# Attention kernel on one core: first loads in halves and earlier, a second load behind a memset, and 64-query pieces ahead of 192-query pieces in one of three score steps

## The chip, the cores and the metric

The program runs on one core of one Trainium2 chip. The metric is device time in microseconds (us) for the whole program. "Span" is the time from the first to the last instruction of the profiled execution; it lies about 1.8 us under the measured time.

## The reference

```python
B, H, Sq, Sk, D = 16, 32, 192, 1024, 128        # q, k, v: bf16, normal * 0.05

def reference(q, k, v):
    scale = q.shape[-1] ** -0.5
    scores = jnp.einsum("bhqd,bhkd->bhqk", q, k) * scale
    p = _softmax(scores, axis=-1)
    return jnp.einsum("bhqk,bhkd->bhqd", p, v)
```

There are 512 heads with 192 queries and 1024 keys each. Reading K, V and q and writing the output moves 319 MB.

## The kernel before

Four heads make a group, so there are 128 groups, numbered x. The 4 x 192 queries times 1024 keys of a group are worked in three steps; a step has a number f, and b = f mod 3 says which third of a group it is. For each group

- SP loads K (1 MB), q (192 KB) and V (1 MB) into one of five buffers each,
- DVE transposes K in three pieces (`turn_k`) and q once, three steps ahead of use,
- POOL reorders the K pieces (`order`) and spreads V (`spread`),
- PE makes the scores (`qk`, row tiles of 32), ACT takes the exponential straight out of PSUM (one activation of 512 columns, here called the exp of step f, then one of 1536), PE makes output and row sum (`pv`, four steps later), and DVE divides (`onorm`).

PE runs the following. `take(s, c)` is an instruction of its own: it waits until a semaphore is c or more and takes c off.

```python
CUTS = (                      # per step: groups of pieces (key tile, first query, last query)
    (((0, 0, 192),), ((1, 0, 192),), ((2, 0, 128),)),
    (((3, 0, 192), (2, 128, 192)), ((4, 0, 192), (5, 0, 64))),      # the middle step, b = 1
    (((5, 64, 192),), ((6, 0, 192),), ((7, 0, 192),)),
)
def qk(f):
    x, b = divmod(f, 3)
    if b == 0:
        take(s_qt, 1)
    take(s_kt, 1)
    take(s_e1, 1)
    for group in CUTS[b]:
        for w in range(4):
            for g, (t, n0, n1) in enumerate(group):
                for a in range(4):
                    ins = pe.matmul(...)          # 32 rows x 128 keys, n1 - n0 queries
    ins.then_inc(s_qk, 1)

def pv(s, part=(0, 32)):
    x, i = divmod(s, 3)
    if part[0] == 0:
        if i == 0:
            take(s_e3, 3)
            take(s_vp, 2)
        ...                                       # last steps cut
            take(s_on, 1)
    for n in range(*part):
        ins = pe.matmul(...)                      # 32 matmuls of 129 columns
    ins.then_inc(s_pv, 1)

with nc.Fori(0, NF // (3 * R), engines=[PE], ...):    # six steps a turn
    pv(-PRE - 1 - LAG, (CLOSE, 32))
    for f in range(-PRE, 3 * R - PRE):
        qk(f)
        pv(f - LAG, (0, CLOSE if f == 3 * R - PRE - 1 else 32))     # LAG = 4
```

`pv` with i = 0 always stands in a step with b = 1. The first steps work on blank data that POOL, DVE and ACT set, until the first K has come. SP starts with two waits, one for the first real score step, one for a blank output step:

```python
load_k(0)
load_k(1)
load_q(e, 1)
for n in range(2, NKN):
    if n == 2:
        e.wait_ge(s_qk, PRE + 1)        # first wait: scores of step 0 are done
    load_v(n - 2)
    if n == 2:
        e.wait_ge(s_pv, BLANK - 2)      # second wait: output matmuls of step 1 are done
    load_k(n)
    load_q(e, n)
for n in range(NQ):                     # ... then V, K, q of the next groups for ever
```

Of the kernel before, what the change touches and what calls it, by code (L numbers as in the profile page):

```python
# [30 lines left out]
def _general_path(nc, q, k, v, out, redo, hints, stored, G=16, NS=2, LAGS=(2, 4, 5, 7), ROUTES=(R_W, R_W, R_EA)):  # L31
# [376 lines left out]
U32 = mybir.dt.uint32  # L408
# [3 lines left out]

CUTS = (
    (((0, 0, 192),), ((1, 0, 192),), ((2, 0, 128),)),
    (((3, 0, 192), (2, 128, 192)), ((4, 0, 192), (5, 0, 64))),
    (((5, 64, 192),), ((6, 0, 192),), ((7, 0, 192),)),
)
PIECES = ((0, 6), (6, 12), (12, 16))
# [2 lines left out]
def _attention_kernel(nc, q, k, v, out):  # L421
# [5 lines left out]
    T = SK // 128  # L427
# [6 lines left out]
    PRE = 1  # L434
    BLANK = LAG + 1 + PRE

    AHEAD = 3
    NKN, NVS, NKT, NVP = 5, 5, 2, 2
# [5 lines left out]
    kf = k.rearrange("b h s d -> (b h) s d")  # L444
    vf = v.rearrange("b h s d -> (b h) s d")
# [5 lines left out]
    with ExitStack() as outer:  # L451
        redo = outer.enter_context(nc.sbuf_tensor("redo", [1, 1], mybir.dt.int32))

        def sem(name):
            return outer.enter_context(nc.semaphore(name))

        s_set = sem("f_set")
        s_one = sem("f_one")
        s_out = sem("f_out")
        s_kn = [sem("f_kn%d" % i) for i in range(NKN)]  # L460
        s_qn = [sem("f_qn%d" % i) for i in range(NKN)]
        s_v = [sem("f_v%d" % i) for i in range(NVS)]
# [5 lines left out]
        s_qk = sem("f_qk")  # L468
        s_e1 = sem("f_e1")
        s_e3 = sem("f_e3")  # L470
        s_pv = sem("f_pv")
# [7 lines left out]
        with ExitStack() as es:  # L479
            def sb(name, shape, dt):  # L480
                return es.enter_context(nc.sbuf_tensor(name, shape, dt))
# [5 lines left out]
            kn = sb("f_kn", [128, NKN, 2048], U32)  # L487
# [7 lines left out]
            vs = sb("f_vs", [128, NVS, 4, T * D], BF16)  # L495
            vp = sb("f_vp", [128, NVP, 4 * T, VB], BF16)
# [17 lines left out]
            def store(e, i):  # L514
                so = i % NSO
                x, c = stores[i]
                if x + c == NQ:
                    e.wait_ge(s_fin, 1)
                else:
                    e.wait_ge(s_rc, 3 * (x + c) + 1)  # L520
                e.dma_start(
                    of[4 * x:4 * x + 4 * c].rearrange("(a x) (p j) d -> (x p) a (j d)", x=2, j=3),
                    ob[:, so, 0:6 * c, :].rearrange("p (a j) d -> p a (j d)", j=3),
                ).then_inc(s_st[so], 16)
# [4 lines left out]
            def load_q(e, x):  # L529
                e.dma_start(  # L530
                    qn[:, x % NKN, :],
                    qf[4 * x:4 * x + 4].rearrange("a (j u) d -> (a j) (u d)", u=6).bitcast(U32),
                ).then_inc(s_qn[x % NKN], 16)
# [3 lines left out]
            def hint(eng):  # L537
                hints[eng.engine] = eng.mark_branch_hint_location()

            @block.sync  # L540
            def _(e):
                def load_k(x):
                    if x >= NKN:
                        e.wait_ge(s_kx, 3 * (x - NKN) + 3)
                    e.dma_start(
                        kn[:, x % NKN, :],
                        kf[4 * x:4 * x + 4].rearrange("a (j r) d -> (a j) (r d)", r=32).bitcast(U32),
                    ).then_inc(s_kn[x % NKN], 16)

                def load_v(x):  # L550
                    if x >= NVS:
                        e.wait_ge(s_pv, 3 * (x - NVS) + 2 + BLANK)
                    e.dma_start(
                        vs[:, x % NVS, :, :],
                        vf[4 * x:4 * x + 4].rearrange("a (m t) d -> m a (t d)", t=T),
                    ).then_inc(s_v[x % NVS], 16)

                load_k(0)
                load_k(1)
                load_q(e, 1)  # L560
                for n in range(2, NKN):

                    if n == 2:
                        e.wait_ge(s_qk, PRE + 1)
                    load_v(n - 2)
                    if n == 2:
                        e.wait_ge(s_pv, BLANK - 2)
                    load_k(n)
                    load_q(e, n)
                for n in range(NQ):  # L570
                    if n == NQ // 2:
                        hint(e)
                    if n + NKN - 2 < NQ:
                        load_v(n + NKN - 2)
                    if n + NKN < NQ:
                        load_k(n + NKN)
                        load_q(e, n + NKN)
                for i in range(len(store_at), len(stores)):
                    store(e, i)
# [4 lines left out]
            @block.gpsimd  # L584
            def _(gp):
                gp.memset(ones[:], 1.0).then_inc(s_one, 1)  # L586

                def set_v(part):
                    return gp.memset(part.bitcast(U32), 0x3F803F80)  # L589

                set_v(vp[:, 0, 0:2 * T].rearrange("p a d -> p (a d)")).then_inc(s_set, 1)
                set_v(vp[:, 0, 2 * T:].rearrange("p a d -> p (a d)")).then_inc(s_out, 1)
                set_v(vp[:, 1].rearrange("p a d -> p (a d)")).then_inc(s_vp, 2)

                def order(g):
                    x, b = divmod(g, 3)
                    lo, hi = PIECES[b]
                    gp.wait_ge(s_kx, g + 1)
                    if x >= NKT - 1 and b == 0:
                        gp.wait_ge(s_qk, 3 * (x - NKT) + 3 + PRE)  # L600
                    gp.tensor_copy(  # L601
                        kt[:, x % NKT].bitcast(U32).rearrange("p U (j s u) c -> p U j s (u c)", s=2, u=2)[:, lo:hi],
                        kx[:, x % 2].rearrange("p (U s j u) -> p U j s u", s=2, j=32, u=2)[:, lo:hi],
                    ).then_inc(s_kt, 1)

                def spread(x, i):
                    if i == 0:
                        gp.wait_ge(s_v[x % NVS], 16 * (x // NVS + 1))
                        gp.wait_ge(s_pv, 3 * (x - NVP) + 3 + BLANK)
                    gp.tensor_copy(  # L610
                        vp[:, x % NVP, 2 * T * i: 2 * T * i + 2 * T, 0:D].bitcast(U32),
                        vs[:, x % NVS, 2 * i: 2 * i + 2, :].rearrange("p a (t d) -> p (a t) d", d=D).bitcast(U32),
                    ).then_inc(s_vp, 1)

                for x in range(NQ + 1):
                    if x == NQ // 2:
                        hint(gp)
                    if x < NQ:
                        for b in range(3):
                            order(3 * x + b)  # L620
                    if x >= 1:
                        for i in range(2):
                            spread(x - 1, i)
# [84 lines left out]
            def _(dve):  # L708
# [10 lines left out]
                for z in range(2):  # L719
                    ins = clear(low[:, z, :, 2, :])  # L720
                ins.then_inc(s_out, 1)
                dve.wait_ge(s_out, 3)
                dve.sem_inc(s_on, LAG + 1 + PRE)
                where = {}
                for i, (x0, c) in enumerate(stores):
# [3 lines left out]
                def turn_k(g):  # L729
                    x, b = divmod(g, 3)  # L730
                    lo, hi = PIECES[b]
                    if b == 0:
                        dve.wait_ge(s_kn[x % NKN], 16 * (x // NKN + 1))
                    if x >= 2:
                        dve.wait_ge(s_qk, 3 * (x - 2) + b + 1 + PRE)
                    dve.transpose(  # L736
                        kx[:, x % 2].rearrange("p (U s j u) -> p s u U j", s=2, j=32, u=2)[:, :, :, lo:hi],
                        kn[:, x % NKN].rearrange("p (s u U i) -> p s u U i", s=2, u=2, i=32)[:, :, :, lo:hi],
                    ).then_inc(s_kx, 1)
# [30 lines left out]
                def check(lo, hi, i, part):  # L770
# [9 lines left out]
                    dve.wait_ge(s_dv, cnt[0])  # L780

                turn_k(0)
                turn_q(0)
                for g in range(1, 5):
                    turn_k(g)
                turn_q(1)
                for f in range(NF + LAG + 1):
                    s = f - LAG - 1
                    if f == NF // 2:
                        hint(dve)  # L790
                    if s >= 0:
                        onorm(s)
                        if 0 <= s - EARLY < 3:
                            check(0, 2 * EARLY, 0, s - EARLY)
                    g = f + AHEAD
                    if 5 <= g < NF:
                        x, b = divmod(g, 3)
                        if b == 2 and x >= 2:
                            turn_q(x)
                        turn_k(g)  # L800
# [37 lines left out]
def bass_standalone__mha_softmax__near_ridge_kernel(  # L838
    nc: bass.Bass,
    q: bass.AP,  # L840
    k: bass.AP,
    v: bass.AP,
    out: bass.AP,
):
    _attention_kernel(nc, q, k, v, out)
# [28 lines left out]
```

## Time and profile before

| | before |
|---|---|
| time, median of 3 runs | 819.46 us (819.17 to 820.69) |
| span of the profiled run | 816.9 us |
| PE busy | 99% |
| steps b = 0, 1, 2 in mid-run | 2.06, 2.10, 2.05 us; 6.218 us for a group |
| DMA, 40 slices | 90% or more of all 16 engines in slices 2 to 39 |

The page of the kernel before opens with the span and then gives busy time by engine. In the rows of its 40-slice part a digit is the busy share of a slice in tenths.

```profile
span 816.9 us, 71709 instructions
PE 806.7 (99%) x32996; PEld 717.5 (88%) x32996; DVE 599.7 (73%) x1293; ACT 749.8 (92%) x772; POOL 550.7 (67%) x648
...
DMA  7999999999999999999999999999999999999992
```

PE and DMA are both full, so either can be the limit. Apart from the last slice, where the loads are over, the start is the only place where both have holes. In the windows view of the kernel before, each line is a stretch of one us with the busy time of PE, weight loads, DVE, ACT and POOL, then the granted TensorE clock, the DMA share and GB/s. The DMA share adds up the times of the packets, so it can pass 1.

```profile
9.00:10.00 1.00, 1.00 (x50) 0.89 (x47) 0.58 (x1) 0.00 (x0) 0.94 (x2) 1.00 0.08 30
10.00:11.00 1.00, 1.00 (x36) 0.91 (x40) 0.76 (x1) 0.96 (x2) 0.49 (x1) 1.00 0.10 23
11.00:12.00 1.00, 1.00 (x66) 0.87 (x64) 1.00 (x2) 0.97 (x1) 0.71 (x1) 1.00 0.89 82
...
14.00:15.00 1.00, 1.00 (x52) 0.84 (x42) 0.00 (x0) 0.16 (x2) 0.00 (x0) 1.00 1.55 377
15.00:16.00 1.00, 1.00 (x43) 0.91 (x40) 0.00 (x0) 1.00 (x2) 0.38 (x1) 1.00 0.39 125
```

The last two figures matter: DMA stands nearly still from 9 to 11 us, starts again slowly, and dips once more at 15 us. The timeline of SP in the kernel before tells why; its columns are start, duration, engine, line, operation, and how many were merged.

```profile
10.03 0.38 SPq L553 DMA_DIRECT2D f_vs<-in_v_dram  x1
13.86 0.33 SPq L545 DMA_DIRECT2D f_kn<-in_k_dram  x1
...
14.71 1.64 SPq L553 DMA_DIRECT2D f_vs<-in_v_dram  x1
16.39 0.51 SPq L545 DMA_DIRECT2D f_kn<-in_k_dram  x1
```

K0 and K1 were issued at 0.81 and 1.26 us. V0 (10.03) and K2 (13.86) are issued behind the two waits. V1 (14.71) and K3 (16.39) come after K2 in program order.

The exp activations in mid-run (timeline of ACT, lines of the 512-column activation; the longer one is left out). Their starts are 2.06 and 2.10 us apart; the second interval is the middle step; a bracket gives the idle time before the instruction and what ended it.

```profile
299.00 0.60 ACT L828 ACTIVATE f_pt<-f_s 128x512 bf16<-128x512 f32 x1
...
301.06 0.60 ACT L828 ACTIVATE f_pt<-f_s 128x512 bf16<-128x512 f32 x1
...
303.16 0.60 ACT L828 ACTIVATE f_pt<-f_s 128x512 bf16<-128x512 f32 x1 [0.16 <-PE f_s L646]
```

Two more lines of the timeline show it:

```profile
26.79 0.42 DVE L761 TENSOR_TENSOR f_ob<-f_o,f_rinv 128x256 bf16<-128x256 f32 x1
...
27.36 1.10 PE L673 MATMUL f_o<-f_vp,f_pt 128*64 128x129 bf16 x32 [1.23 <-PEq L629]
```

### The profile page before, as it was taken

How to read it: one execution, taken by the hardware profiler on the slowest of the kernel's cores; microseconds unless marked ns; L12 is line 12 of the kernel's file. 1: busy time of each engine (PE TensorE's matmuls, PEld its weight loads, DVE VectorE, ACT ScalarE, POOL GpSimd, SP SyncE). 2: the span in 40 equal slices, each digit the busy share in tenths (PEclk: the TensorE clock that was granted, in tenths of full speed). 3: DMA queues.
4: the chain of work that ended last, by engine and by line, in shares of the span. 5: the costliest groups of instructions: out<-in, count | busy, mean ns of one | idle time of the engine just before them, and what ended most of it. 6: DMA issues, size and time to landing. Idle time of an engine off the chain costs nothing. (4 is left out here: it accounts for less than half of the span.)

```text
span 816.9 us, 71709 instructions
## 1 busy us (share of the span) xinstructions
PE 806.7 (99%) x32996; PEld 717.5 (88%) x32996; DVE 599.7 (73%) x1293; ACT 749.8 (92%) x772; POOL 550.7 (67%) x648
## 2 busy tenths in 40 slices
PE   8999999999999999999999999999999999999997
PEld 6888888888888888888888888888888888888886
DVE  4777777777777777777777777777777777777775
ACT  6899999999999999999999999999999999999995
POOL 5667766766776676677667666766766676676664
PEclk9999999999999999999999999999999999999999
DMA  7999999999999999999999999999999999999992
GB/s 269 401 402 405 410 403 406 408 403 406 409 401 407 408 403 409 408 402 409 407 403 408 407 403 407 405 405 400 397 406 403 382 411 397 389 404 387 402 368 70
DMA packets 138294, 319.16 MB, mean 391 GB/s; under 512 B 7184, under 2 KB 56336, under 8 KB 121872
## 3 DMA queue, kind: packets, MB, share of 16 engines
q1 hardware_dynamic: 105376, 294.22, 91.9%
q10 hardware_dynamic: 32880, 24.58, 9.0%
q14 instruction: 32, 0.26, 0.1%
q8 instruction: 6, 0.10, 0.0%
HBM read 293.60 MB, written 25.17 MB: 390 GB/s over the span
## 5 line engine op out<-in xcount | busy, mean ns | idle before, releaser
L831 ACT ACTIVATE f_pt<-f_s 128x1536 bf16<-128x1536 f32 x384 | 554.9, 1445 | 0.0
L601 POOL COPY f_kt<-f_kx 128x768 uint32<-128x768 uint32 (+1 forms) x384 | 301.0, 784 | 254.2 <-DVE f_kx L736 254.1
L673 PE MATMUL f_o<-f_vp,f_pt 128*64 128x129 bf16 x12368 | 425.8, 222 | 2.9 <-PEq L629 1.9
L646 PE MATMUL f_s<-f_qt,f_kt 32*128 32x192 bf16 (+1 forms) x20528 | 423.2, 226 | 2.4 <-PEq L629 1.8
L673 PEld LDWEIGHTS f_o<-f_vp,f_pt 128*64 128x64 bf16 x12368 | 366.1, 110 | 55.2 <-issue 28.1
L646 PEld LDWEIGHTS f_s<-f_qt,f_kt 32*128 32x128 bf16 x20528 | 348.5, 92 | 38.9 <-issue 3.1
L736 DVE STREAM_TRANSPOSE f_kx<-f_kn 128x768 uint32<-128x768 uint32 (+1 forms) x384 | 334.0, 870 | 15.7 <-DMA f_kn<-in_k_dram 15.3
L828 ACT ACTIVATE f_pt<-f_s 128x512 bf16<-128x512 f32 x384 | 229.3, 597 | 58.7 <-PE f_s L646 25.6
L610 POOL COPY f_vp<-f_vs 128x1024 uint32<-128x1024 uint32 x256 | 259.9, 1045 | 1.8 <-DMA f_vs<-in_v_dram 1.8
L757 DVE RECIPROCAL f_rinv<-f_o 128x2 f32<-128x2 f32 x381 | 64.9, 170 | 183.2 <-PE f_o L673 183.0
L761 DVE TENSOR_TENSOR f_ob<-f_o,f_rinv 128x256 bf16<-128x256 f32 x381 | 161.7, 424 | 13.3 <-DVE f_rinv L757 0.3
L745 DVE STREAM_TRANSPOSE f_qt<-f_qn 128x384 uint32<-128x384 uint32 x128 | 73.1, 571 | 0.0
L814 ACT ACTIVATE f_pt<-f_ones 128x1536 f32<-128x1536 bf16 x3 | 4.2, 1472 | 0.0
L589 POOL MEMSET f_vp<- 128x1088 uint32 (+1 forms) x3 | 3.8, 1309 | 0.0
L673 PE MATMUL f_s<-f_vp,f_pt 128*64 128x129 bf16 x96 | 3.1, 220 | 0.2 <-PEq L629 0.2
L673 PEld LDWEIGHTS f_s<-f_vp,f_pt 128*64 128x64 bf16 x96 | 2.9, 110 | 0.3 <-issue 0.3
L814 ACT ACT_TABLE_LOAD x1 | 1.3, 1283 | 1.2 <-PEq L859 1.2
L686 PE MATMUL f_o<-f_ones 128*128 128x512 bf16 x2 | 1.0, 622 | 1.1 <-POOL f_ones L586 1.1
L710 DVE MEMSET f_pt<- 128x256 uint32 x4 | 1.1, 272 | 0.9 <-PEq L859 0.9
L703 PE MATMUL f_o<-f_bad,f_ones 128*1 128x1 bf16 x1 | 0.2, 164 | 1.3 <-DVEq L803 1.3
L757 DVE RECIPROCAL f_rinv<-f_s 128x2 f32<-128x2 f32 x3 | 0.5, 170 | 1.2 <-PE f_s L673 1.2
L703 PEld LDWEIGHTS f_o<-f_bad,f_ones 128*1 128x1 bf16 x1 | 0.1, 79 | 1.4 <-DVEq L803 1.4
(15 smaller groups left out, 6.5 us busy)
## 6 DMA issues: line engine op xcount, KB each, us to landing
f_kn<-in_k_dram SPq DMA_DIRECT2D x128, 1024.0 KB, 18.1
f_vs<-in_v_dram SPq DMA_DIRECT2D x128, 1024.0 KB, 16.3
f_qn<-in_q_dram SPq DMA_DIRECT2D x127, 192.0 KB, 14.2
out_dram<-f_ob ACTq DMA_DIRECT2D x62, 384.0 KB, 9.5
out_dram<-f_ob SPq DMA_DIRECT2D x1, 384.0 KB, 3.1
out_dram<-f_ob SPq DMA_DIRECT2D x2, 192.0 KB, 2.0
f_qn<-in_q_dram ACTq DMA_DIRECT2D x1, 192.0 KB, 5.2
```

The source lines that it names most:

```text
L589: return gp.memset(part.bitcast(U32), 0x3F803F80)
L601: gp.tensor_copy(kt[:, x % NKT].bitcast(U32).rearrange("p U (j s u) c -> p U j s (u c)", s=2, u=2)[:, lo:hi], kx[:, x % 2].rearrange("p (U ...
L610: gp.tensor_copy(vp[:, x % NVP, 2 * T * i: 2 * T * i + 2 * T, 0:D].bitcast(U32), vs[:, x % NVS, 2 * i: 2 * i + 2, :].rearrange("p a (t d) ...
L646: ins = pe.matmul(S[:, c0: c0 + n1 - n0], kt[r, x % NKT, 2 * t + h, :, c], qt[r, x % R, h, n0:n1, c], start=w == 0 and g == 0, stop=w == 3 ...
L673: ins = pe.matmul(O[64 * z: 64 * z + 64, u, 0:129], pt[:, x % R, 2 * y + z, t * SQ + 64 * j: t * SQ + 64 * j + 64], vp[:, x % NVP, (2 * y ...
L736: dve.transpose(kx[:, x % 2].rearrange("p (U s j u) -> p s u U j", s=2, j=32, u=2)[:, :, :, lo:hi], kn[:, x % NKN].rearrange("p (s u U i) ...
L745: dve.transpose(qt[:, x % R].bitcast(U32).rearrange("p b (y j u) c -> p u y b (j c)", y=3, u=2), qn[:, x % NKN].rearrange("p (u y b i) -> ...
L757: dve.reciprocal(ri, O[:, :, 128]).then_inc(s_rc, 1)
L761: dve.tensor_tensor(ob[:, so, 6 * a + 2 * w: 6 * a + 2 * w + 2, :], O[:, :, 0:128], ri.unsqueeze(2).to_broadcast([128, 2, D]), ALU.mult,). ...
L814: return act.activation(part.bitcast(F32), ones[:, 0:1].to_broadcast([128, 2 * T * SQ // 2]), ACT_FN.Copy)
L828: act.activation(pt[:, x % R, 0, c], s1_ps[:], ACT_FN.Exp, scale=scale).then_inc(s_e1, 1)
L831: act.activation(pt[:, x % R, 1:4, c], s3_ps[f % 2][:], ACT_FN.Exp, scale=scale).then_inc(s_e3, 1)
```

## The change

The intent is to fill the holes in the load stream at the start (half of V0 and half of K2 come earlier), to keep K0 alone in the queue until POOL has set a blank buffer, and to end the middle step's scores on a long piece. Cut to its core:

```diff
-    (((3, 0, 192), (2, 128, 192)), ((4, 0, 192), (5, 0, 64))),
+    (((2, 128, 192), (3, 0, 192)), ((5, 0, 64), (4, 0, 192))),
...
                 load_k(0)
+                e.wait_ge(s_blank, 1)
                 load_k(1)
                 load_q(e, 1)
-                for n in range(2, NKN):
-                    if n == 2:
-                        e.wait_ge(s_qk, PRE + 1)
+                load_v(0, 0, 2)
+                e.wait_ge(s_qk, PRE + 1)
+                load_v(0, 2, 4)
+                load_k(2, 0, 16)
+                e.wait_ge(s_pv, BLANK - 2)
+                load_k(2, 16, 32)
+                load_q(e, 2)
+                for n in range(3, NKN):
                     load_v(n - 2)
-                    if n == 2:
-                        e.wait_ge(s_pv, BLANK - 2)
                     load_k(n)
                     load_q(e, n)
...
-                        gp.wait_ge(s_v[x % NVS], 16 * (x // NVS + 1))
+                        gp.wait_ge(s_v[x % NVS], 16 * (x // NVS + (2 if x % NVS == 0 else 1)))
...
-                        dve.wait_ge(s_kn[x % NKN], 16 * (x // NKN + 1))
+                        dve.wait_ge(s_kn[x % NKN], 16 * (x // NKN + (2 if x % NKN == 2 else 1)))
```

The last two pairs count one more load in V0's and K2's buffers. The number of matmuls stays, and so does their work.

More of the change, by code (lines that the diff above doesn't have):

```diff
@@ L459, in _attention_kernel @@
         s_out = sem("f_out")
+        s_blank = sem("f_blank")
         s_kn = [sem("f_kn%d" % i) for i in range(NKN)]
@@ L541, in _, with load_k @@
             def _(e):
-                def load_k(x):
+                def load_k(x, lo=0, hi=32):
                     if x >= NKN:
@@ L545, in load_k, with load_v @@
                     e.dma_start(
-                        kn[:, x % NKN, :],
-                        kf[4 * x:4 * x + 4].rearrange("a (j r) d -> (a j) (r d)", r=32).bitcast(U32),
+                        kn[:, x % NKN, 64 * lo:64 * hi],
+                        kf[4 * x:4 * x + 4].rearrange("a (j r) d -> (a j) r d", r=32)[:, lo:hi, :]
+                        .rearrange("p r d -> p (r d)").bitcast(U32),
                     ).then_inc(s_kn[x % NKN], 16)
-                def load_v(x):
+                def load_v(x, lo=0, hi=4):
                     if x >= NVS:
@@ L553, in load_v @@
                     e.dma_start(
-                        vs[:, x % NVS, :, :],
-                        vf[4 * x:4 * x + 4].rearrange("a (m t) d -> m a (t d)", t=T),
+                        vs[:, x % NVS, lo:hi, :],
+                        vf[4 * x + lo:4 * x + hi].rearrange("a (m t) d -> m a (t d)", t=T),
                     ).then_inc(s_v[x % NVS], 16)
                 load_k(0)
+                e.wait_ge(s_blank, 1)
                 load_k(1)
                 load_q(e, 1)
-                for n in range(2, NKN):
-                    if n == 2:
-                        e.wait_ge(s_qk, PRE + 1)
+                load_v(0, 0, 2)
[6 more added lines that the diff above has]
+                for n in range(3, NKN):
                     load_v(n - 2)
-                    if n == 2:
-                        e.wait_ge(s_pv, BLANK - 2)
                     load_k(n)
@@ L591, in _ @@
                 set_v(vp[:, 0, 0:2 * T].rearrange("p a d -> p (a d)")).then_inc(s_set, 1)
-                set_v(vp[:, 0, 2 * T:].rearrange("p a d -> p (a d)")).then_inc(s_out, 1)
+                set_v(vp[:, 0, 2 * T:].rearrange("p a d -> p (a d)")).then_inc(s_blank, 1)
                 set_v(vp[:, 1].rearrange("p a d -> p (a d)")).then_inc(s_vp, 2)
@@ L721, in _ @@
                 ins.then_inc(s_out, 1)
-                dve.wait_ge(s_out, 3)
+                dve.wait_ge(s_out, 2)
+                dve.wait_ge(s_blank, 1)
                 dve.sem_inc(s_on, LAG + 1 + PRE)
```

## The prediction

> **What bounds the kernel now.** Engine summary: PE busy 99% of 816.9 us; 40-slice view: DMA 90% or more in slices 2 to 39. Two limits nearly coincide. PE: a group of four heads takes 6.218 us (spacing of the exp activations; steps 2.06, 2.10, 2.05 us). DMA: K lands every 6.20 us, every 6.3 us after about 620 us. Landings against the transposes that read them (DMA issues, timeline): K0 to K4 are read within 0.03 us of landing, in mid-run K lies 0.5 to 1.9 us, from K104 on often 0.02 us again. K's issue ends at least 6 us after its buffer is free, so the queue is full, not held by semaphores. So loads pace the start (to 37 us) and the end (from 650 us); PE paces the middle, at most 2 us behind. The span is the load stream plus 20.7 us after K127 (796.15 us). The Trainium skill, "DMA: Bandwidth & Descriptors", section "Issuing engines are not separate DMA queues": all queues share 16 engines; 92% for loads plus 9% for stores agrees.
>
> **What the change does.**
> 1. Early halves. In 1-us windows DMA falls to 30, 23, 82 GB/s from 9 to 12 us and 125 GB/s at 15 us: V0 is issued at 10.03 us (after the first score step), K2 at 13.86 us, each at full rate only 2 us later. About 3.5 us of transfer are lost. After: half of V0 (0.5 MB, 1.3 us at 400 GB/s) follows q1 without a gap; half of K2 follows V0's rest. Only K2's second half keeps a gap of about 1 us. Saved: 1.2 to 2.5 us.
> 2. K1 issued at 2.9 instead of 1.26 us. K0's packets start until 5.7 us and K1's follow, so K1 loses nothing; K0 may land 0 to 0.7 us before 6.67.
> 3. 64 before 192 in the middle step. A pair costs 113 ns either way. At the end, the next matmul starts 185 ns after a 64-query group (which costs about 29), but 182 ns after a 192-query one (85), so ending with 192 hides about 50 ns. Middle scores: 1.084 us now, 1.018 and 1.034 in the other steps. Estimate: 2.10 falls to 2.05 us, 128 x 0.05 = 6 us of PE time.
>
> **On the critical path.** Item 3 alone gives little: DMA then paces everything, and the 6 us become waits for K. It lets PE stand closer to the last K: tail shorter by 0 to 1 us. Item 1 shifts the whole load stream and counts in full; item 2 only through the first score step. Sum: 2 + 0.3 + 0.5, about 2.7 us.
>
> **Predicted: 816.8 us, 80% range 814.4 to 818.8.** Faster by over 2%: 1%; within 2%: 98%; slower: 1%.
>
> **What shows each step.** Right: DMA over 200 GB/s between 9 and 11 us; K2 lands at about 17.5 instead of 19.41 us; K5 and K127 land 1.5 to 3.5 us earlier; the middle step takes 2.04 to 2.06 us where PE isn't starved; yet the period stays about 6.21 us, DVE's wait for K rises from 15.3 to about 20 us, and K is read within 0.05 us of landing for most of the run. Wrong: K127 unmoved; period 6.17 us.
>
> **What would make it wrong.** PE's instruction fetches (16 KB at 7.1, 10.7, 14.8 us, 1.1 us each) share the DMA engines; V0's early half may lengthen PE's 0.7 us stalls near 13 and 17 us. The stream's slow last third may vary. If loads have headroom that the full queue hides, the order gives up to 6 us.

## More of the kernel before

A bracket gives the idle time before the instruction and what ended it.

```profile
25.72 0.98 DVE L736 STREAM_TRANSPOSE f_kx<-f_kn 128x768 uint32<-128x768 uint32 x1 [2.02 <-DMA f_kn<-in_k_dram]
...
29.53 0.60 ACT L828 ACTIVATE f_pt<-f_s 128x512 bf16<-128x512 f32 x1 [1.42 <-PE f_s L646]
```

DVE waits 2.02 us for K3, and 3.8 us after its arrival the exp of step 8 starts, after a hole in PE's work. Step 8 does not use K3 itself. But DVE works in program order, and the division of an earlier step stands behind the transpose that waits for K3; PE's next output matmuls take the semaphore of that division (`s_on`; L629 is the take), and the scores of step 8 come after them.

## The result, and the profile after

| | before | after |
|---|---|---|
| time, median of 4 runs | 819.32 us (818.60 to 820.69) | 820.32 us (817.96 to 820.58) |
| span of the profiled run | 816.9 us | 816.2 us |
| group in mid-run | 6.218 us | 6.218 us |
| middle step | 2.10 us | 2.10 us |
| K2, K3, K127 landed | 19.41, 25.70, 796.15 us | 18.08, 25.13, 795.75 us |

The ratio of the times is 1.0004, with a 95% interval of 0.9981 to 1.0026. Ratios here are the mean time of one kernel's fast runs over that of the other's of the same rounds, so they are not quite the ratio of the medians. There is no gain. The predicted 816.8 us, and its range up to 818.8 us, are missed.

The page after reads the same but for the span:

```profile
span 816.2 us, 71711 instructions
PE 806.6 (99%) x32996; PEld 717.7 (88%) x32996; DVE 599.8 (73%) x1293; ACT 750.3 (92%) x772; POOL 551.0 (68%) x648
```

The windows view of the changed kernel at the start, with the columns of before:

```profile
9.00:10.00 1.00, 1.00 (x36) 0.85 (x24) 0.17 (x1) 0.00 (x0) 1.00 (x2) 0.50 0.95 368
10.00:11.00 1.00, 1.00 (x25) 0.95 (x20) 0.75 (x1) 0.76 (x2) 0.07 (x1) 0.50 0.17 54
11.00:12.00 1.00, 1.00 (x28) 0.82 (x26) 1.00 (x2) 1.00 (x1) 0.71 (x1) 0.50 0.52 147
...
14.00:15.00 1.00, 1.00 (x56) 0.91 (x50) 0.00 (x0) 1.00 (x1) 0.63 (x1) 1.00 0.47 180
15.00:16.00 1.00, 1.00 (x42) 0.84 (x33) 0.00 (x0) 0.84 (x3) 1.00 (x2) 1.00 0.57 188
```

The first hole is partly filled (368 instead of 30 GB/s from 9 to 10 us), but the second has grown: 180 and 188 GB/s from 14 to 16 us where the kernel before had 377 and 125. Summing the bytes of the load queue's packets, the changed kernel is 0.66 MB ahead at 13 us. At 0.385 MB/us (that queue moves 0.40 MB/us from 26 to 40 us and 0.37 later) this is a lead of 1.7 us, and at 20 us only 0.6 us are left. That lead of 0.6 us stays to the end (0.69 us at 780 us). The timeline of SP in the changed kernel shows what did not move:

```profile
3.79 6.75 SPq L555 DMA_DIRECT2D f_vs<-in_v_dram  x2
10.58 4.01 SPq L546 DMA_DIRECT2D f_kn<-in_k_dram  x2
...
15.11 1.20 SPq L555 DMA_DIRECT2D f_vs<-in_v_dram  x1
16.35 0.51 SPq L546 DMA_DIRECT2D f_kn<-in_k_dram  x1
```

The merged durations include the waits. K3 is issued at 16.35 us, against 16.39 us before.

The middle step in mid-run is as long as before (timeline of ACT, starts 2.06 and 2.10 us apart):

```profile
298.44 0.60 ACT L835 ACTIVATE f_pt<-f_s 128x512 bf16<-128x512 f32 x1
...
300.50 0.60 ACT L835 ACTIVATE f_pt<-f_s 128x512 bf16<-128x512 f32 x1
...
302.60 0.60 ACT L835 ACTIVATE f_pt<-f_s 128x512 bf16<-128x512 f32 x1 [0.16 <-PE f_s L652]
```

And K3's arrival and the exp of step 8 (timelines of DVE and ACT) keep their distance of 3.8 us, 0.57 us earlier than before:

```profile
25.15 0.98 DVE L743 STREAM_TRANSPOSE f_kx<-f_kn 128x768 uint32<-128x768 uint32 x1 [1.51 <-DMA f_kn<-in_k_dram]
...
28.97 0.60 ACT L835 ACTIVATE f_pt<-f_s 128x512 bf16<-128x512 f32 x1 [0.91 <-PE f_s L652]
```

The granted clock differs from the profile before: 0.50 from 9 to 12 us, in the trace exactly one stretch of 3.41 us from 8.82 us on. It makes the interval between the exps of steps 0 and 1 3.03 instead of 2.08 us. The Trainium skill, "TensorE: Matmul & The Clock Gate", section "What's actually happening", describes it: the clock is halved after an idle window, and the window of about 3.4 us is free-running. The length of 3.41 us agrees. An idle window does not: in the 3.41 us before the halved stretch PE was busy for 1.29 us. The profiles also show that the halved stretch does not come with the new loads: two profiles with the old loads have one of 3.41 us too (from 8.27 and 8.49 us on), and one with the new loads (`loads_only`) has none. That the phase of the window decides is the skill's account; no run here shows it.

### The profile page after: what moved, and what is told of

It reads as the page before. It is cut to its first block, busy times and chain, and to the rows that moved or that the text cites. A ratio compares the mean times of both kernels' runs of the same rounds, so it can differ in the third digit from the quotient of the medians.

```text
span 816.2 us, 71711 instructions
## 1 busy us (share of the span) xinstructions
PE 806.6 (99%) x32996; PEld 717.7 (88%) x32996; DVE 599.8 (73%) x1293; ACT 750.3 (92%) x772; POOL 551.0 (68%) x648
## 5 line engine op out<-in xcount | busy, mean ns | idle before, releaser
L743 DVE STREAM_TRANSPOSE f_kx<-f_kn 128x768 uint32<-128x768 uint32 (+1 forms) x384 | 334.1, 871 | 15.2 <-DMA f_kn<-in_k_dram 14.6
L768 DVE TENSOR_TENSOR f_ob<-f_o,f_rinv 128x256 bf16<-128x256 f32 x381 | 161.8, 425 | 13.3 <-DVE f_rinv L764 0.3
```

The lines of the kernel that those rows point to most:

```text
L743: dve.transpose(kx[:, x % 2].rearrange("p (U s j u) -> p s u U j", s=2, j=32, u=2)[:, :, :, lo:hi], kn[:, x % NKN].rearrange("p (s u U i) ...
L768: dve.tensor_tensor(ob[:, so, 6 * a + 2 * w: 6 * a + 2 * w + 2, :], O[:, :, 0:128], ri.unsqueeze(2).to_broadcast([128, 2, D]), ALU.mult,). ...
```

## The experiments

Twelve kernels ran, all with correct results and five rounds each, next to the kernel before on the same chip. The medians of before were 819.27, 819.11 and 819.38 us in the three sets. The theories:

- A: the load stream sets the time; the change wins a little lead there, and nothing on PE, because the middle step's extra length is a chain of semaphore takes.
- B: the change really costs about 1 us, as the first medians say.
- Other rivals: the order of the pieces sets the middle step; loads have headroom; early loads starve PE's instruction fetches; PE sets the time.
- C, after the first two sets: up to step 8, K3's landing sets PE's position; from there PE's own chain runs to the end, unless loads are slower.

### The changed kernel again: `after_again`

No edit.

> The changed kernel once more, to see its sign with more rounds. Theory A (the load stream sets the time, the change wins about 0.6 us of transfer lead and nothing on PE): ratio 0.998 to 1.000. Theory B (the change really costs about 1 us, as the medians 820.32 against 819.32 say): ratio 1.001 to 1.002. The profile tells whether the halved clock between 8.8 and 12.2 us, seen in the first profile of it, comes with the change (seen again)[...].

Measured: 819.76 us, ratio 1.0002 (0.9986 to 1.0018). With the first run of it, there is no change to within 0.3%. Theory B's 1 us (0.12%) lies inside both intervals, so the times alone do not exclude it. A halved clock was there again, from 9.72 us. Bytes by 13 us: 1.87 us ahead; by 20 us 0.2 us ahead. K3 was issued at 16.91 and landed at 26.41 us, no earlier than before's.

### Only the order of the pieces: `order_only`

```diff
-    (((3, 0, 192), (2, 128, 192)), ((4, 0, 192), (5, 0, 64))),
+    (((2, 128, 192), (3, 0, 192)), ((5, 0, 64), (4, 0, 192))),
```

> The kernel before with only the order of the pieces in the middle step changed. Theory A (the middle step's extra 50 ns is the chain of three semaphore takes ahead of its output matmuls, not the order): middle step stays at 2.10 us, period 6.218 us, ratio 0.999 to 1.001. Theory of the prediction (order sets it): middle step 2.05 us.

Measured: 819.49 us, ratio 1.0007 (0.9988 to 1.0026); middle step 2.10 us, group 6.213 us. The order does nothing. From the start of its score matmuls to the start of its output matmuls the middle step takes 1.075 us here and 1.077 us in the kernel before (medians of 90 steps), although the last score matmul starts 0.218 us ahead of them here and 0.160 us there: the output matmuls start at the same time whichever piece ends the scores. So they wait for something else.

### Only the loads: `loads_only`

```diff
# the changed kernel with
-    (((2, 128, 192), (3, 0, 192)), ((5, 0, 64), (4, 0, 192))),
+    (((3, 0, 192), (2, 128, 192)), ((4, 0, 192), (5, 0, 64))),
```

> The changed loads with the old order of the pieces. Theory A: everything that the change does is here: bytes loaded by 13 us are about 0.6 MB more than before's (a lead of 1.5 us or more), of which 0.5 to 1 us is left by 25 us and stays to the end; ratio as of after_again, 0.998 to 1.000. Rival: the order matters too and this is slower than after_again by 0.3% or more.

Measured: 819.40 us, ratio 1.0003 (0.9986 to 1.0020). The lead is 1.95 us at 13 us, 0.66 us at 20 us, 0.8 to 1.1 us from 22 us to the end: as expected, and still not seen in the time, whose interval is wider than it. This profile has no halved clock at the start, and its second stop ended early (K2's second half issued at 12.93 us, against 14.25 us in the changed kernel), yet K3 landed at 25.34 us, no earlier than the changed kernel's 25.13. So the halved clock does not explain the missing gain.

### The take of the exp semaphore moved: `take_moved`

The records of PE's semaphore instructions show what stands between scores and output. In the kernel before, around the steps that begin at 298 us:

```
start us   length ns   semaphore taken
298.627    51          s_on                     step b = 0: output matmuls start at 298.873
300.573    51          s_e3
300.728    51          s_vp
300.879    51          s_on                     step b = 1: output matmuls start at 300.987
302.791    51          s_on                     step b = 2: output matmuls start at 303.035
```

In the middle step three takes stand in a row, about 0.15 us apart, and the output matmuls start 57 ns after the end of the last. In the other steps the one take is done 0.2 us ahead. One of the three can stand earlier without weakening anything, since an earlier wait is the stricter one:

```diff
 def qk(f):
     ...
     take(s_e1, 1)
+    if b == 1:
+        take(s_e3, 3)
 def pv(s, part=(0, 32)):
     ...
         if i == 0:
-            take(s_e3, 3)
+            if s == NF - 3:          # the last one has no score step of its own
+                take(s_e3, 3)
             take(s_vp, 2)
```

> The kernel before, with the take of the exp semaphore moved from just ahead of the middle step's output matmuls to ahead of its score matmuls, where the queue covers it. Theory A (three takes of about 0.15 us in a row make the middle step 50 ns longer): middle step falls from 2.10 to 2.05 us where PE is not starved. And since the load stream then paces the run, the period falls only to about 6.20 us and the time by 0 to 1.5 us (ratio 0.998 to 1.000). Rival 1 (the 64-query tail sets the middle step): middle step stays at 2.10. Rival 2 (loads have headroom): period 6.17 us and the time falls by 5 to 6 us (ratio 0.993).

Measured: 817.46 us, ratio 0.9983 (0.9964 to 1.0001), whose interval just reaches 1. From scores to output the middle step takes 1.033 us instead of 1.077. The middle step is 2.05 us (timeline of ACT of this kernel, three starts 2.06 apart):

```profile
297.67 0.60 ACT L831 ACTIVATE f_pt<-f_s 128x512 bf16<-128x512 f32 x1
...
299.73 0.60 ACT L831 ACTIVATE f_pt<-f_s 128x512 bf16<-128x512 f32 x1
...
301.79 0.60 ACT L831 ACTIVATE f_pt<-f_s 128x512 bf16<-128x512 f32 x1
```

The group takes 6.173 us for the first 64 groups (400 us), and 6.17 to 6.26 us after them (means of eight groups). From K44 on, the smallest distance from landing to use in every six K is 0.02 us. So the takes were the cause of the 50 ns, and once they are gone the loads hold the kernel in its second half. The waits of DVE for K from 400 to 790 us (waits view: us in total, times, longest) are where the gain goes:

```profile
DVE f_kx L739 <- DMA f_kn<-in_k_dram: 26.3, 48, 1.4
```

In the kernel before the same view has 2.8 us in 7 waits from 31 us to the end.

### No waits at the start: `no_waits`

```diff
# the kernel before with
-                    if n == 2:
-                        e.wait_ge(s_qk, PRE + 1)
                     load_v(n - 2)
-                    if n == 2:
-                        e.wait_ge(s_pv, BLANK - 2)
                     load_k(n)
```

> The kernel before with both waits of the start taken out: V0 and K2 are issued right behind q1, as whole loads into buffers that nothing else uses yet. Theory A (the load stream sets the end, a lead won at the start stays): about 1.0 to 1.5 MB more loaded by 20 us, a lead of 2.5 to 3.5 us that is still there at 780 us; K127 lands 2 to 3.5 us earlier; ratio 0.996 to 0.998. Rival (the waits are there because early loads starve the instruction fetches): PE stalls longer between 9 and 25 us, the lead is lost by 40 us or PE ends later, ratio 1.000 or more.

Measured: 823.34 us, ratio 1.0053 (1.0040 to 1.0066): slower, as the rival said. The loads are 4.3 us ahead at 20 us and 4.8 us at 780 us, and K127 lands at 788.33 instead of 796.15 us, yet the span is 4.7 us longer. This ends theory A as it stood. PE loses its time at the start; the timeline of PE shows the longest hole:

```profile
18.02 0.98 PE L642 MATMUL f_s<-f_qt,f_kt 32*128 32x192 bf16 x38
22.25 0.34 PE L642 MATMUL f_s<-f_qt,f_kt 32*128 32x128 bf16 x10 [3.25 <-issue]
```

The same place in the kernel before:

```profile
15.81 0.97 PE L646 MATMUL f_s<-f_qt,f_kt 32*128 32x192 bf16 x38
17.27 0.34 PE L646 MATMUL f_s<-f_qt,f_kt 32*128 32x128 bf16 x10 [0.50 <-issue]
```

"issue" means that PE waited for nothing that the profile shows. The DMA records show it: packets of 16,384 bytes on the instruction queue, about 1 us each. The third of them ran from 14.83 to 15.98 us in the kernel before, and from 19.80 to 20.90 us here. In both, PE goes on 1.3 us after its end. In all fourteen profiles that distance is 1.24 to 1.45 us. After the fourth (until 22.20 us in the kernel before) this queue is empty until 807 us. The Trainium skill, "Runtime: NRT & Kernel Launch", section "Instruction fetch mechanics", says that the sequencer fetches blocks of 16 KiB (256 instructions) through its own DMA queue; the packet size agrees. It calls the cost mostly hidden; in this trace it is not, in the first turn of the loop.

### No waits, and the take moved: `no_waits_take`

Both edits above together.

> The same with the exp take moved ahead of the middle step's score matmuls. Theory A: lead of the loads as of no_waits, and PE no longer holds the middle of the run, so the lead shows in full: ratio 0.994 to 0.997, lower than take_moved's 0.9983 and than no_waits. Rival: no better than take_moved.

Measured: 818.41 us, ratio 0.9987 (0.9974 to 1.0000): 4.9 us faster than `no_waits`, though it carries the same stalls. The group takes 6.173 us through the whole run. With K at least 7 us early from K8 on, this is PE alone. So the PE chain is worth nearly the full 128 x 0.045 = 5.8 us wherever loads do not hold it. The expected ratio (0.994 to 0.997) was missed for the stalls at the start.

### No second stop ahead of K2: `k2_free`

```diff
# the changed kernel with
                 load_k(2, 0, 16)
-                e.wait_ge(s_pv, BLANK - 2)
                 load_k(2, 16, 32)
```

> The changed kernel without the wait ahead of K2's second half, so that only V0's second half and K2 wait, for the first score step, and there is no second stop of the queue. Theory A (the lead of 1.7 us at 13 us is lost at this second stop between 14 and 17 us): the lead at 13 us is as of the changed kernel and stays at 1.5 us or more from 20 to 780 us, instead of 0.2 to 1.0; ratio 0.998 to 0.999. Rival (the lead is lost to something else, such as V1 or instruction fetches): lead falls to under 1 us by 25 us all the same.

Measured: 821.85 us, ratio 1.0036 (1.0023 to 1.0049). The lead is 1.2 us at 20 us and about 1.5 us from 22 to 100 us (4.6 us at 780 us), more than the 0.6 us of the changed kernel, so the second stop does cost lead. K3, though issued at 13.32 us, still landed only at 25.48 us. But the third instruction fetch ends at 19.34 instead of 15.94 us, and PE stalls (timeline of PE):

```profile
15.35 0.98 PE L651 MATMUL f_s<-f_qt,f_kt 32*128 32x192 bf16 x38
20.66 0.34 PE L651 MATMUL f_s<-f_qt,f_kt 32*128 32x128 bf16 x10 [4.32 <-issue]
```

The stop that the change keeps is what lets the fetch through.

### V0 held back: `late_loads`

```diff
# the kernel before with
-                        e.wait_ge(s_qk, PRE + 1)
+                        e.wait_ge(s_qk, PRE + 2)
```

> The kernel before with V0 held back by one more score step (about 2 us). Theory A: about 1 to 1.5 us of transfer are lost by 20 us and stay lost to 780 us; ratio 1.001 to 1.002. Rival (PE sets the time, loads only have to be there): lead negative at 20 us but no longer by 100 us, ratio 1.000.

Measured: 821.32 us, ratio 1.0024 (1.0010 to 1.0037). The loads are 2.4 us behind at 20 us and 1.3 to 2.4 us behind later. K3 lands at 28.29 us, 2.6 us after the kernel before's, and the span is 2.9 us longer. The exp of step 8 starts 3.83 us after K3's landing here, as in the kernel before. But the run does not show that late loads alone cost this: its third instruction fetch was late too (18.07 to 19.14 us), PE stalled for 3.05 us, and steps 3 to 7 were 3.1 to 3.2 us late before K3 came. At step 8 PE then waited only 0.65 us for DVE. Without the later K3, by this profile, about 1.9 of the 2.6 us at step 8 would have stayed.

### The change with the take moved: `after_take` and `loads_take`

The changed kernel with the take moved, and the same with the old order.

> The changed kernel (loads and order) with the exp take moved as in take_moved. Theory C (the end is K3's landing plus 3.84 us to the exp of step 8, plus the PE chain from there; the PE chain is 6.17 us a group with the take moved, until the loads hold it): middle step 2.05 us, the exp of step 8 starts 3.84 us after K3 has landed, ratio 0.996 to 0.999, within 0.001 of take_moved's 0.9983. With the take moved the order could show: rival, this order makes the middle step 2.00 us or less.

> The changed loads with the old order and the take moved. Theory C: same as after_take within 0.1%, middle step within 15 ns of after_take's. Rival (with the take out of the way the order counts): slower than after_take by 0.4% or more, as 50 ns a group would be 6 us.

Measured: `after_take` 818.88 us, ratio 0.9990 (0.9967 to 1.0013); `loads_take` 818.51 us, ratio 0.9983 (0.9965 to 1.0002). With the take out of the way the order shows at last: scores to output 1.024 us against 1.033 us, a group 6.160 against 6.173 us. That is 9 to 13 ns a group, a quarter of what was predicted, and the times do not tell the two apart. The profile of `loads_take` was a slow one for loads (K127 at 799.72 us, span 820.0 us). In `after_take` the exp of step 8 came 4.52 us after K3, not 3.84, with a halved clock from 29.8 us on; that expectation was missed, and the halved clock is a cause that was only argued.

### The second stop ahead of V1: `v1_wait` and `v1_wait_take`

```diff
# the changed kernel with
-                e.wait_ge(s_pv, BLANK - 2)
                 load_k(2, 16, 32)
                 load_q(e, 2)
+                e.wait_ge(s_pv, BLANK - 2)
```

The second kernel has the old order and the moved take besides.

> The changed kernel with the second wait moved from ahead of K2's second half to ahead of V1. K2 then comes whole behind V0, and the pause of the queue still stands where the third instruction fetch is due. Theory C: K3 lands about 1 us sooner than in the changed kernel (24 to 24.7 us), PE's stall near 16 us stays under 1 us, the exp of step 8 starts 3.84 us after K3 lands, ratio 0.998 to 0.9995. Rival (any load in the queue at 12 to 14 us delays the fetch): stall of 2 us or more as in k2_free, step 8 set by PE and not by K3, ratio 1.002 or more.

> The same with the old order and the exp take moved: the candidate for the best. Theory C: v1_wait's gain at the start plus take_moved's 0.17%: ratio 0.9955 to 0.998. Rival: no better than take_moved (0.998 to 1.000).

Measured: `v1_wait` 820.86 us, ratio 1.0016 (0.9999 to 1.0033). K3 landed at 24.88 us, but PE stalled for 3.78 us as in `k2_free`, and step 8 came 7.3 us after K3: the rival's case, though its ratio of 1.002 or more was just missed. `v1_wait_take` 817.26 us, ratio 0.9972 (0.9955 to 0.9989): the lowest median, against 819.38 us of before, the only one whose interval lies under 1, and not told apart from `take_moved`'s 0.9983. Its stall was 1.77 us.

## Why the prediction was wrong

**The time.** Predicted 816.8 us; measured 820.32 us, with a ratio of 1.0004 and again 1.0002. The sum was 2 us of load stream, 0.3 us of an earlier K0 and 0.5 us of tail.

**The order of the pieces: the wrong cause.** The step that failed: "ending with 192 hides about 50 ns". The 185 ns after the last 64-query group were read as that group's uncovered tail. They were the end of three takes, 0.15 us apart. `order_only` leaves the middle step at 2.10 us, `take_moved` brings it to 2.05 us. The order is worth 0 with the takes in place and 9 to 13 ns without them. The prediction's other half, that 6 us won on PE would turn into waits for K, held: `take_moved` wins 1.8 us at the median out of 5.8 us (its interval reaches 1; that the takes cost time is clear from `no_waits` and `no_waits_take`, whose intervals lie apart).

**The loads: the lead was real, and K3 did not get it.** The step that failed: "Only K2's second half keeps a gap of about 1 us. Saved: 1.2 to 2.5 us." Five profiles with the new loads (both of the change, `loads_only`, `after_take`, `loads_take`) can be set against three with the old (before, `order_only`, `take_moved`), by the mean busy share of the 16 DMA engines:

| stretch | old loads | new loads | worth |
|---|---|---|---|
| 9 to 12 us | 0.19 | 0.69 | +1.5 us |
| 12 to 14 us | 0.95 | 0.91 | -0.1 us |
| 14 to 16 us | 0.79 | 0.50 | -0.6 us |
| 16 to 20 us | 1.02 | 0.93 | -0.4 us |
| K2 landed | 20.05 us | 18.74 us | 1.3 us earlier |
| K3 landed | 26.11 us | 25.99 us | 0.1 us earlier |

Worth is the difference of the shares times the length of the stretch. K2 comes 1.3 us sooner, which is its early half, and K3 does not. Two things took the lead. First, V1 and K3 are issued behind the same second wait: K3 at 16.39, 16.75 and 16.75 us with the old loads, at 16.35, 16.91, 17.05 and 16.80 us with the new ones but for `loads_only` (14.28). The queue also runs dry for longer at the stop (a share of 0.50 against 0.79 from 14 to 16 us). Second, the issue is not all: in `loads_only`, `k2_free` and `v1_wait` K3 was issued at 13.3 to 14.3 us and still landed at 24.9 to 25.5 us. A load has landed when all 16 increments of its semaphore are there. In the trace the middle one of K3's comes at 24.66 us with the old loads and at 23.99 with the new ones, 0.7 us earlier, about as the bytes say; the last one comes at 26.11 and 25.99 us. In `k2_free`, without the stop, the middle one comes at 23.03 and the last at 25.48 us. So the last part of K3 lost what the others had won, and DVE waits for the last. Why it trails by 2.0 instead of 1.45 us, and why the queue fills more slowly from 16 to 20 us, is open. The stop could not go either: without it the instruction fetch comes 3.4 us later (`k2_free`).

**What bounds the kernel: half wrong.** The step that failed: "The span is the load stream plus 20.7 us after K127." In the nine profiles with the old takes the span ends 770.1 to 771.2 us after the exp of step 16, while K127 lands anywhere from 788.3 to 797.8 us. So from step 16 on PE's own chain sets the end. The short distances from landing to use after K104 were read as PE being held, but DVE transposes three steps ahead of PE, and a DVE that waits 0.5 us for K holds nobody: from 650 to 800 us its waits for K were 2.6 us in all in the kernel before (waits view):

```profile
DVE f_kx L736 <- DMA f_kn<-in_k_dram: 2.6, 6, 0.8
```

What the loads do set is where PE stands at step 8. In eight of the fourteen profiles the exp of step 8 starts 3.83 to 3.84 us after K3 lands; in five (`k2_free`, `no_waits` and `v1_wait`, with or without the take moved) it comes 7 to 14 us after, set by the fetch stalls, and the last is `after_take`. So the prediction's item 1 would have counted as far as it moved K3 without delaying a fetch. The Trainium skill's statement that loads and stores issued by different engines share the same 16 DMA engines ("DMA: Bandwidth & Descriptors", section "Issuing engines are not separate DMA queues") agrees with the page of the kernel before, where loads take 91.9% and stores 9.0% of their time. It does not speak of instruction fetches; that loads hold these up is what the runs here show (3.4 us in `k2_free`), and the prediction named it only as a risk.

**K0 and K1: inside the range, perhaps by luck.** K0 landed at 6.26 us instead of 6.67, within the 0 to 0.7 us given. But other profiles of the old loads have 6.37 and 6.18 us, so even that is not clearly the change's.

**Shown or not.** DMA over 200 GB/s from 9 to 11 us: once in two windows (368 and 54). K2 at 17.5 us: 18.08. K5 and K127 earlier by 1.5 to 3.5 us: no (37.12 against 37.09 us; 795.75 against 796.15 us). Period about 6.21 us: yes, but not for the reason given. DVE's wait for K up to 20 us: no, 14.6 us.

## What to carry to other kernels

Before a gap ahead of an instruction is put down to the work before it, look at the semaphore instructions between them, and test by changing that work: if the next start does not move, the work was not the cause. A lead in bytes won early in a queue is worth nothing if the transfer that the slow engine really waits for (here K3, and of it the last part) keeps its time, so ask which one that is and whether the change moves it. Where two limits lie within 1%, moving one of them wins at most the distance to the other, and a wait that looks useless may be what lets another transfer, such as an instruction fetch, through.

## What the Trainium skill lacked or had wrong

- "Runtime: NRT & Kernel Launch", "Instruction fetch mechanics", calls a crossing of a 16 KiB block mostly hidden. In the first turn of a long loop, next to a full load queue, it was not: PE stalled for 3.25 us (`no_waits`) and 4.32 us (`k2_free`), and went on 1.24 to 1.45 us after the packet's end. No page says that data loads delay such fetches.
- "TensorE: Matmul & The Clock Gate", "What's actually happening", has the clock halved after an idle window. Near the start of these profiles PE was busy for 0.31 to 1.64 us of the 3.41 us before each of the 16 halved stretches, so a window that is only partly idle was enough.
- No page gives the cost of a run of semaphore takes on PE: a record of 51 ns each, about 0.15 us from one to the next, and 45 ns of each 6.2 us group lost where three stood in a row behind 64 matmuls.
- "DMA: Bandwidth & Descriptors", "Specifications", gives about 0.6 us to the first byte for loads issued from SP. Here V0's first packet started 0.7 us after SP's issuing instruction had ended (10.41 to 11.11 us), which is near it, and 1.1 us after that instruction had started (10.03 us); the page does not say from where it counts. The queue reached 300 GB/s only 2 us after the start of the issue, of which that section says nothing.
- No page tells of a load rate that changes within a run: in the profile of before K landed every 6.22 us from K16 to K96 and every 6.28 us from there to K127, though each K was issued at least 5.2 us after its buffer was free, so that the queue and not the buffers set the pace; `order_only` has 6.21 and 6.27. `no_waits` (6.20 and 6.21) is no contrast, since there each K is issued 0.8 us after its buffer is free, at PE's pace. Why is open.
